# Three reorderings in a one-core spectral filter + MLP kernel: the load order of the row table, a subtraction given to GpSimd, and a copy put ahead of two splits

## The chip, the cores and the metric

The kernel runs on one core of a Trainium2 chip. The metric is the device time of one execution in microseconds (us), median over runs. The engines are TensorE (PE; its weight loads are shown apart as PEld), VectorE (DVE), ScalarE (ACT), GpSimd (POOL) and SyncE (SP, which here only issues DMAs). Each runs its own instruction queue in order and waits on semaphores for the others.

## What is computed

The input is x with 2048 rows (positions) of 576 features. A GFNet filter with a residual is followed by an MLP with a residual:

```python
def _A_ref(x, w_r, w_i):
    B, S, D = x.shape
    X = rfft2(x) * (w_r + 1j * w_i)
    return irfft2(X, s=(S, D))

def _B_ref(x, w1, w2):
    h = jnp.maximum(jnp.einsum("bsd,df->bsf", x, w1), 0)
    return jnp.einsum("bsf,fd->bsd", h, w2)

h = x + _A_ref(_layernorm(x), w_r, w_i)
h2 = h + _B_ref(_layernorm(h), w1, w2)      # w1 576 x 4608, w2 4608 x 576
```

## The kernel before

The work is laid out as one program whose order is written by hand: the tile framework runs in a manual schedule (L171), so that each engine gets its instructions in the order of the Python code, and only the semaphores between engines are worked out for it. x stands in 16 tiles of 128 rows. Matmuls run in a reduced fp32 form; where full precision is needed, an operand is split into a high part (a copy by ACT, L159) and a low part (a subtraction, v minus its high part), and three products are summed.

**Start and forward transform.** `load_x(xs, t, 1)` (L165 to L167) loads one tile in two halves: SP issues both, but for tiles 0 and 1 ACT issues the second. After tiles 0 and 1 SP loads the row table (`cc`, its first 192 columns, `caf` in the code, L173 to L176), then tiles 2 to 15 and the other tables. The first layer norm is folded in. Per tile, DVE makes the statistics (`stat1`, L242; `aggr1`, L246; `row1`, L250 and L251; `add1`, L263), POOL the power for 1/sqrt (`pow1`, L255) and one subtraction (L258), ACT scales the row table by it (`scale1`, L267 and L268), and PE multiplies (`fwd_a`).

**Inverse transform, second layer norm, projection and the first MLP steps.** These are interleaved by the string STEPS, one letter a call: `h` and `d` are the first matmuls of the inverse for a tile (their PSUM is folded by L159 on ACT and L536, L537 on DVE), `o` writes the folded rows (L543 on POOL, L544 on DVE), `r` is its row step, which takes two tiles together (r7 reads tiles 12 and 13), `e` adds the residual (L519, DVE), `s` and `n` are the second layer norm (statistics L215, L216 on DVE, L218 to L221 on POOL), and `j` is `project`. `A` is the first MLP product (A0 and A1 the two halves of its step 0), `B` the second. The part that matters reads

```python
"... j0 j1 h9 d8 s5 r4 n2 e6 o8 e7 d9 o9 j2 j3 h10 d10 r5 h11 e8 s6 e9 s7 s8 "
"n4 o10 d11 s9 o11 j4 A0 j5 h12 n6 A1 d12 r6 h13 e10 e11 d13 o12 j6 j7 B0 B1 o13 B2 =K0 s10 h14 n8 r7 ..."
```

`project(t)` transposes the normalised tile (PE, L564) into a PSUM bank. ACT copies the bank twice (both by L159): its high part into `dst`, the operand buffer of a chunk of four tiles (slots 0 to 5), and all of it into an SBUF buffer `zt`, which SP stores (L572). POOL subtracts twice for the low parts (L574, from `zt`, slots 6 to 9). 576 is 4 x 128 + 64, and the 64 left-over features stand in slot 2: rows 0 to 63 the high part, rows 64 to 127 the low part, made by L575 on DVE from the PSUM bank. After the fourth tile of a chunk SP copies rows of slot 2 to slot 5 within SBUF (L579, four copies: the first two read rows 32 to 63, the last two rows 96 to 127) and then rows 0 to 31 to rows 32 to 63 of slot 2 (L580). A product such as A0 has 14 matmuls; its last two read the slots 2 and 5.

PSUM has four wide banks in two pools of two; a string `order` says from which pool each new bank comes. A bank is free again when its last reader is done.

**Doubles.** From about 280 us the MLP runs as Strassen-Winograd products on pairs of chunks and weight groups. `slot(d)` has seven rounds r: PE makes one product of the next double's first layer (`l1_prod`, L825), and two products of this double's second layer (`second`, L930), whose results DVE adds (L940). Between them, `pieces` runs what the table PLAN names for a round and a place: `u2c` copies the first-layer bank into SBUF (ACT), `y1h` and `y1l` are the high and low part of the sums s1, s2 (ACT L159, DVE L839; the sums are made on POOL, L845 to L851), `y3h` and `y3l` the same of s3, s4. `weights(d, r)` splits and loads weights for the next turn: `w1_split("A2", nc.gpsimd)` has two copies on ACT (high and rest) and two subtractions on POOL (L353, L377), and `load_w1` issues DMAs. In the first double (d = 0, `late`) there is a plan of its own for the rounds 0 to 2.

Of the kernel before, what the change touches and what calls it, by code (L numbers as in the profile page):

```python
# [129 lines left out]
def kernel(ctx: ExitStack, tc: tile.TileContext, x, w_r, w_i, w1, w2, cc2, c1, fb, ib, c3, out):  # L130
    nc = tc.nc
# [6 lines left out]
    def sb(shape, tag, bufs=1, dt=F32):  # L138
        n[0] += 1
        return pool.tile(shape, dt, tag=tag, name=f"{tag}_{n[0]}", bufs=bufs)  # L140
# [6 lines left out]
    def ps():  # L147
        n[0] += 1
        return (wide if next(order) == "w" else psum).tile([128, 1024], F32, tag="d", name=f"d_{n[0]}", bufs=2)

    def ebuf(shape, dt=F32):
        e = sb([128, EW], "e", EB, dt)[:, :int(np.prod(shape[1:]))]
        return e.rearrange("p (a b) -> p a b", a=shape[1]) if len(shape) == 3 else e
# [4 lines left out]
    def act(o, i, **kw):  # L158
        nc.scalar.activation(o, i, AF.Copy, **kw)  # L159

    xs = sb([128, NT, D], "X")
# [3 lines left out]
    def load_x(xs, t0, k):  # L165
        for j in range(2):
            (nc.scalar if j and t0 < 2 else nc.sync).dma_start(xs[64 * j:64 * j + 64, t0:t0 + k, :], xv[j, :, t0:t0 + k, :])  # L167
# [2 lines left out]
    make_identity(nc, ident)  # L170
    ctx.enter_context(tc.manual_schedule())  # L171
    load_x(xs, 0, 1)
    load_x(xs, 1, 1)  # L173
    ccs = sb([128, 320], "cc")
    caf, cai = ccs[:, :192], ccs[:, 192:]
    nc.sync.dma_start(caf, cc2[:, :192])  # L176
    for i in range(2, NT):
        load_x(xs, i, 1)
    cst = ebuf([128, 1160])
# [151 lines left out]
    def load_w1(g, v1, v4):  # L331
        f = slice(256 * g, 256 * g + 256)
        nc.sync.dma_start(v1, w1[0:512, f].rearrange("(a p) f -> p a f", p=128))
        for k in range(3):
            nc.sync.dma_start(v4[32 * k:32 * k + 32], w1[512:576, f].rearrange("(h p) f -> p h f", p=32))
# [135 lines left out]
    xs = xa[:, :NT * D].rearrange("p (t d) -> p t d", t=NT)  # L471
# [88 lines left out]
    def project(t):  # L560
        y = Zs.pop(t)
        pz = ps()
        for b in range(5):
            nc.tensor.transpose(pz[:, 128 * ORDER[b]:128 * ORDER[b] + 128], y[:, 128 * b:128 * b + 128], ident)  # L564
        q = slice(128 * (t % CH), 128 * (t % CH) + 128)
        dst = xc[t // CH]
        pzv = pz[:, :640].rearrange("p (a s) -> p a s", s=128)
        act(dst[:, 0:5, q], pzv)
        zt = ebuf([128, 640])
        act(zt, pz[:, :640])  # L570
        xd[t] = dram.tile([128, 640], F32, name=f"x{t}")
        nc.sync.dma_start(xd[t], zt)  # L572
        for h in range(2):
            nc.gpsimd.tensor_sub(dst[:, 6 + 2 * h:8 + 2 * h, q], zt[:, 384 * h:384 * h + 256].rearrange("p (a s) -> p a s", s=128), dst[:, 3 * h:3 * h + 2, q])  # L574
        nc.vector.tensor_sub(dst[64:, 2, q], pzv[64:, 2], dst[64:, 2, q])  # L575
        if t % CH == CH - 1:
            u = dst.bitcast(F32)
            for a, b in ((0, 32), (32, 32), (64, 96), (96, 96)):
                nc.sync.dma_start(u[a:a + 32, 5], u[b:b + 32, 2])  # L579
            nc.sync.dma_start(u[32:64, 2], u[0:32, 2])  # L580
# [126 lines left out]
    def load_sum(p, n, back=False):  # L707
        if back:
            td[p, n] = dram.tile([128, 2560], F32, name=f"t{p}{n}")
        for at, v, m in zip((0, 384) if n != "B22" else (0, 1536), TF[n], (3, 2)):  # L710
            v = v.rearrange("p a n -> p (a n)").bitcast(F32)
            t = td[p, n][:, at:at + 512 * m]
            if n != "B22":
                v, t = v.rearrange("p (j n) -> p j n", j=4), td[p, n].rearrange("p (j n) -> p j n", j=4)[:, :, at:at + 128 * m]
            nc.sync.dma_start(*((t, v) if back else (v, t)))
# [37 lines left out]
    def w1_split(n_, eng):  # L753
        v, s_, v4 = vs[1], vs["s"], vs[4]
        if n_ == "A11":
            split(*W1["A11"][:2], v[:, 0:2, :128], eng)
            split_rest(W1["r"][:, 768:896], v4[:, 0, :128], nc.gpsimd)
        elif n_ == "A2":
            split(*(v2d(x) for x in W1["A2"]), v[:, 2:4, :], eng)
            split_rest(W1["r"][:, 512:768], v4[:, 1], eng)  # L760
        else:
            k = n_ == "S34"
            split(*W1[n_], s_[:, 512 * k:512 * k + 512], eng)
            split_rest(W1["r"][:, 256 * k:256 * k + 256], vs["r"][k], eng)
# [9 lines left out]
    def w2_sums():  # L774
        v, s_ = vs[2], vs["s"]
        b11, b12, b21, b22 = v[:, 0, :288], v[:, 0, 288:], v[:, 1, :288], v[:, 1, 288:]
        t1, t2, t3, t4 = (s_[:, 288 * k:288 * k + 288] for k in range(4))
        nc.gpsimd.tensor_sub(t1, b12, b11)
        nc.gpsimd.tensor_sub(t2, b22, t1)
        nc.gpsimd.tensor_sub(t3, b22, b12)  # L780
        nc.gpsimd.tensor_sub(t4, b21, t2)

    def w2_split(n_, eng):
        v, s_ = vs[2], vs["s"]
        if n_ == "B1":
            split(*W2["B1"], v[:, :, :288], eng)
        elif n_ == "B22":
            split(*W2["B22"], v[:, 1, 288:], eng)
        else:
            k = 576 * (n_ == "T34")  # L790
            split(*W2[n_], v2d(s_[:, k:k + 576]), eng)
# [16 lines left out]
    LAST = len(doubles) - 1  # L808
# [18 lines left out]
    def piece(d, n_):  # L827
# [73 lines left out]
    PLAN = {  # L901
# [7 lines left out]
    }  # L909
    PRE = "z3h yAh yc2"  # L910

    def pieces(d, names, first=False):
        for n_ in names.split():
            if first and (n_[0] == "y" or n_ in ("z1h", "z1l", "z3l")):
                continue
            piece(d, n_)
# [50 lines left out]
    def weights(d, r):  # L967

        g = doubles[max(d, 0)][0]
        turn = (d + 1) % 2  # L970
        if not turn and r == 0 and d > 0:
            w2_split("T34", nc.vector)
            w2_split("B22", nc.gpsimd)
        if g == NG - 1:
            return
        if turn:
            if r == 1:
                w1_split("A2", nc.gpsimd)
                if g + 2 < NG:
                    load_w1(g + 2, vs[1], vs[4])  # L980
            if r == 3:
                w2_sums()
            if r == 4:
                w2_split("B1", nc.gpsimd)
            if r == 5:
                w2_split("T12", nc.gpsimd)
            for n_, k in STREAM:
                if max(k, 2 * (d == 0)) == r:
                    load_sum(doubles[d + 2][1], n_)
        else:  # L990
            if r == (1 if d > 0 else 5):
                load_w2(g + 1, vs[2])
            if r == 1:
                w1_split("A11", nc.gpsimd)
            early = d < 0
            if r == 2 - early:
                w1_sums(0)
            if r == 3 - early:
                w1_sums(1)
            if r == 4 - early:  # L1000
                w1_split("S12", nc.gpsimd)
            if r == 5 + early:
                w1_split("S34", nc.gpsimd)

    def slot(d):
        pieces(d, PRE if d else "")
        late = not d
        for r in range(7):
            l1_prod(d + 1, (0, 2, 1)[r] if late and r < 3 else r)
            plan = PLAN.get((r, 0), "")  # L1010
            if late:
                plan = {0: "p1c z1h z1l", 1: "", 2: "u2c"}.get(r, plan)
            pieces(d, plan)
            if not late or r:
                second(d, 2 * r - late)
            pieces(d, PLAN.get((r, 1), ""))
            second(d, 2 * r + 1 - late)
            if late and r == 0:
                pieces(d, PRE)
            if late and r == 2:  # L1020
                split(*HF["Y"]["A11"], fx["p1"][0][:, :256])
            if late and r == 6:
                second(d, 13)
            pieces(d, PLAN.get((r, 2), "").replace("yBh yBl", "" if d == LAST - 1 else "yBh yBl"))
            weights(d, r)
            if d == LAST - 1 and r == 4:
                split(W1["S12"][0][:, :288], W1["S12"][1][:, :288], vs[2][:, 0, 288:], eng=nc.gpsimd)
            if d == LAST - 1 and r == 5:
                split(*HF["Y"]["S12"], fx["p1"][LAST % 2], eng=nc.gpsimd)
# [148 lines left out]
    for d in range(LAST):  # L1178
        slot(d)
# [23 lines left out]
```

## Time and profile before

| | us |
|---|---|
| median of 3 runs | 971.03 (971.01 to 971.31) |
| the profiled execution | 971.31 |
| its span, first to last instruction | 969.3 |
| PE busy in the span | 957.8 |
| DVE, ACT, POOL busy | 780.2, 464.4, 633.2 |

A row of the timeline gives start and duration in us, engine, line, operation, output <- input by buffer names, shapes, a count where neighbours were drawn together, and in brackets the idle time ahead of it with what ended it. A group's row gives busy us and mean ns, then the idle us ahead. A row with q behind the engine (SPq) is its DMA queue: the time that issuing took, not the transfer.

### The profile page before, as it was taken

What the parts mean: (1) busy time and instruction counts of PE and PEld (TensorE: products, weight loads), DVE (VectorE), ACT (ScalarE), POOL (GpSimd) and SP (SyncE); (2) the same over time, 40 slices, a digit from 0 to 9 for tenths busy, and PEclk for the clock granted to TensorE, in tenths of its full rate; (3) what the DMA queues carried; (4) which work ended last, traced back from release to release, by engine and by line L of the source; (5) the groups of instructions that cost most, each with busy time, mean ns of one, the idle gap of its engine ahead of it and who ended that gap; (6) DMA issues with size and microseconds to landing.
All of it is one profiled execution on the core that took longest, in us unless ns stands there. A gap on an engine that the chain in (4) does not pass through costs nothing.

```text
span 969.3 us, 18102 instructions
## 1 busy us (share of the span) xinstructions
PE 957.8 (99%) x6658; PEld 849.5 (88%) x6658; DVE 780.2 (80%) x1235; ACT 464.4 (48%) x912; POOL 633.2 (65%) x774
## 2 busy tenths in 40 slices
PE   8999999999999999999999999999999999999998
PEld 7777678899988999999999999999999999999997
DVE  8677976787858888888888888888888888888886
ACT  6544556333345454545454544444454554544441
POOL 7213755623777866777776878776777777686842
PEclk9999999999999999999999999999999999999999
DMA  7874735567559182645637181927355472809265
GB/s 208 227 191 111 176 102 192 184 221 250 199 167 313 45 295 84 242 144 183 202 124 264 63 301 43 308 65 262 122 204 181 147 242 84 298 30 325 95 216 158
DMA packets 122840, 176.09 MB, mean 182 GB/s; under 512 B 7552, under 2 KB 102400, under 8 KB 122752
## 3 DMA queue, kind: packets, MB, share of 16 engines
q1 hardware_dynamic: 121584, 173.61, 55.3%
q10 hardware_dynamic: 1168, 1.33, 0.4%
q8 instruction: 53, 0.87, 0.4%
q14 instruction: 35, 0.29, 0.1%
HBM read 150.53 MB, written 23.07 MB: 179 GB/s over the span
## 4 chain that ended last, share of the span: by engine, by line
PE 92%; DVE 4%; issue 1%; POOL 1%; ACT 1%; DMA 0%; DVEq 0%; POOLq 0%; ACTq 0%
PE h L825 35%; PE d L930 34%; PE d L156 22%; DVE A L519 1%; DVE st L215 1%; PE d L564 1%; DVE st L242 1%; PE h L930 0%; DVE e L536 0%; DVE e L537 0%; DMA X<-in_A_x_dram 0%; ACT e L159 0%; ACT X L159 0%; DVE X L544 0%; POOL e L353 0%
## 5 line engine op out<-in xcount | busy, mean ns | idle before, releaser
L940 DVE TENSOR_TENSOR A<-A,d 128x576 f32<-128x576 f32 x428 | 316.8, 752 | 80.1 <-PE d L930 67.7
L930 PE MATMUL d<-X,D 128*128 128x288 f32 x1476 | 224.2, 294 | 0.1
L930 PEld LDWEIGHTS d<-X,D 128*128 128x128 f32 x1476 | 211.0, 188 | 10.5 <-DVE A L940 0.3
L825 PE MATMUL h<-B,e 128*128 128x512 f32 x658 | 166.8, 392 | 0.0
L159 ACT ACTIVATE e<-h 128x512 f32<-128x512 f32 x93 | 55.6, 598 | 184.8 <-PE h L825 184.8
L825 PEld LDWEIGHTS h<-B,e 128*128 128x128 f32 x658 | 118.3, 188 | 20.3
L353 POOL TENSOR_TENSOR e<-e,e 128x512 fp32r<-128x512 f32 (+4 forms) x67 | 89.0, 1328 | 58.9 <-ACT e L159 58.8
L825 PE MATMUL h<-X,e 128*128 128x512 f32 x434 | 110.2, 393 | 1.0 <-ACT e L159 1.0
L641 ACT ACTIVATE e<-e 128x512 f32<-128x512 f32 x93 | 58.9, 634 | 105.8 <-DVE e L883 47.0
L353 POOL TENSOR_TENSOR X<-e,X 128x576 fp32r<-128x576 f32 (+1 forms) x34 | 50.0, 1471 | 63.7 <-ACT X L159 63.0
L825 PEld LDWEIGHTS h<-X,e 128*128 128x128 f32 x434 | 78.0, 188 | 14.6 <-ACT e L159 1.2
L159 ACT ACTIVATE e<-e 128x256 fp32r<-128x256 f32 (+5 forms) x171 | 78.8, 490 | 17.3 <-DVE e L672 6.1
L849 POOL TENSOR_TENSOR A<-e 128x256 f32<-128x256 f32 x61 | 48.1, 788 | 28.0 <-DVE X L839 19.9
L839 DVE TENSOR_TENSOR D<-A,D 128x512 fp32r<-128x512 f32 x61 | 64.8, 1062 | 1.7 <-ACT D L159 1.7
L930 PEld LDWEIGHTS d<-X 128*128 128x128 f32 x372 | 55.6, 188 | 5.3 <-issue 0.4
L930 PE MATMUL d<-X 128*128 128x288 f32 x372 | 58.9, 294 | 0.1
L930 PE MATMUL d<-X,e 128*128 128x288 f32 x360 | 57.1, 294 | 0.0
L825 PE MATMUL h<-F,e 128*128 128x512 f32 x217 | 55.0, 392 | 0.0
L156 PE MATMUL d<-e,D 128*128 128x288 f32 x384 | 53.3, 295 | 0.0
L825 PE MATMUL h<-C,e 128*128 128x512 f32 x210 | 53.3, 392 | 0.0
L851 POOL TENSOR_TENSOR A<-e,A 128x256 f32<-128x256 f32 x61 | 52.7, 863 | 0.8 <-DVE A L847 0.8
L156 PEld LDWEIGHTS d<-e,D 128*128 128x128 f32 x384 | 51.9, 188 | 1.3 <-issue 0.4
(174 smaller groups left out, 1850.6 us busy)
## 6 DMA issues: line engine op xcount, KB each, us to landing
X<-t0T SPq DMA_DIRECT2D x16, 768.0 KB
X<-t1T SPq DMA_DIRECT2D x16, 768.0 KB
e<-in_B_w_dram SPq DMA_DIRECT2D x18, 576.0 KB
e<-in_B_w_dram SPq DMA_DIRECT2D x18, 512.0 KB
X<-t0T SPq DMA_DIRECT2D x16, 512.0 KB
X<-t1T SPq DMA_DIRECT2D x16, 512.0 KB
B<-t1T SPq DMA_DIRECT2D x8, 768.0 KB
B<-t1B SPq DMA_DIRECT2D x8, 768.0 KB
```

Source lines behind the costliest of these rows:

```text
L156: nc.tensor.matmul(o, l, r, start=start, stop=stop)
L159: nc.scalar.activation(o, i, AF.Copy, **kw)
L215: nc.vector.bn_stats(st[:, i, h, :], xs[:, t0 + i, 288 * h:288 * h + 288])
L242: nc.vector.bn_stats(first(t)[2][:, h, :], xs[:, t, 288 * h:288 * h + 288])
L353: eng.tensor_sub(l, v, h)
L641: nc.scalar.activation(o, i, AF.Relu)
L825: nc.tensor.matmul(o, a, b, start=bool(first) and n_ == 0, stop=n_ == len(ops) - 1, skip_group_check=not first)
L839: (eng or nc.vector).tensor_sub(f[1], v, f[0])
L849: nc.gpsimd.tensor_sub(s3, p0[:, :256], p0[:, 256:])
L851: nc.gpsimd.tensor_sub(s4, p1_[:, :256], s2)
L930: nc.tensor.matmul(P[tt], l[:, q], r, start=first and n_ == 0, stop=end and n_ == 2, skip_group_check=whole and not first)
L940: nc.vector.tensor_add(xt, xt, P)
```

## The change

Three edits that compute the same values.

1. SP issues the row table ahead of tile 1's half, no longer behind it.
2. `project`'s L575 takes its input from the SBUF copy `zt` instead of the PSUM bank, for all 16 tiles; for tiles 0 to 7 it runs on POOL instead of DVE.
3. In the first double, `w1_split("A2")` (with `load_w1` behind it) moves from the end of round 1 to the end of round 2, and `y1h y1l` from the end of round 1 to round 2, behind `u2c`.

```diff
     load_x(xs, 0, 1)
-    load_x(xs, 1, 1)
     ccs = sb([128, 320], "cc")
     caf, cai = ccs[:, :192], ccs[:, 192:]
     nc.sync.dma_start(caf, cc2[:, :192])
+    load_x(xs, 1, 1)
...
-        nc.vector.tensor_sub(dst[64:, 2, q], pzv[64:, 2], dst[64:, 2, q])
+        (nc.gpsimd if t < 8 else nc.vector).tensor_sub(dst[64:, 2, q], zt[64:, 256:384], dst[64:, 2, q])
...
-            if r == 1:
+            if r == (1 if d else 2):
                 w1_split("A2", nc.gpsimd)
...
-                plan = {0: "p1c z1h z1l", 1: "", 2: "u2c"}.get(r, plan)
+                plan = {0: "p1c z1h z1l", 1: "", 2: "u2c y1h y1l"}.get(r, plan)
...
-            pieces(d, PLAN.get((r, 2), "").replace("yBh yBl", "" if d == LAST - 1 else "yBh yBl"))
+            if not late or r != 1:
+                pieces(d, PLAN.get((r, 2), "").replace("yBh yBl", "" if d == LAST - 1 else "yBh yBl"))
```

What this does to the queues, at two places. POOL in the projection, tiles 2 and 3 (e_1704 and e_1718 are their `zt`, B_1416 is `dst`), with the engine semaphores that each row waits for:

```order
 L574 TENSOR_TENSOR B_1416<-e_1704,B_1416 128x2x128 [waits Activation_49]
 L574 TENSOR_TENSOR B_1416<-e_1704,B_1416 128x2x128
-L574 TENSOR_TENSOR B_1416<-e_1718,B_1416 128x2x128 [waits Activation_49]
+L575 TENSOR_TENSOR B_1416<-e_1704,B_1416 64x128 [waits Pool_49]
+L574 TENSOR_TENSOR B_1416<-e_1718,B_1416 128x2x128 [waits Activation_49,Pool_49]
 L574 TENSOR_TENSOR B_1416<-e_1718,B_1416 128x2x128
-L218 TENSOR_SCALAR r_1761<-mv_1760 128x2 [waits DVE_49]
+L575 TENSOR_TENSOR B_1416<-e_1718,B_1416 64x128 [waits Pool_49]
+L218 TENSOR_SCALAR r_1761<-mv_1760 128x2 [waits DVE_49,Pool_49]
 L219 TENSOR_TENSOR r_1761<-r_1761,half_169 128x2 [waits Pool_49]
```

Each tile's L575 now stands behind its two L574 and waits for POOL's own earlier work; what follows on POOL stands behind it. The eight rows of L575 are gone from DVE's queue.

ACT in the first double (h_3270 is the bank that u2c, e_3208, copies; D_3422<-A_1399 is y1h; e_3205 and e_3206 are the two copies of the split A2; e_3420<-e_3208 is the split of A11 and e_3420<-A_1399 is y3h):

```order
 L641 ACTIVATE e_3295<-h_3269 128x512
-L159 ACTIVATE D_3422<-A_1399 128x512
-L159 ACTIVATE e_3205<-e_2775 128x512
-L159 ACTIVATE e_3206<-G_2777 128x256
-L159 ACTIVATE e_3208<-h_3270 128x512
-L159 ACTIVATE e_3420<-e_3208 128x256
-L159 ACTIVATE e_3420<-A_1399 128x512
+L159 ACTIVATE e_3208<-h_3270 128x512
+L159 ACTIVATE D_3422<-A_1399 128x512
+L159 ACTIVATE e_3420<-e_3208 128x256
+L159 ACTIVATE e_3420<-A_1399 128x512
+L159 ACTIVATE e_3205<-e_2775 128x512
```

The copy u2c went ahead of y1h, and the two copies of the split (e_3206 follows e_3205) behind y3h. PE, DVE and POOL have the same order there as before.

## The prediction, made before the change was run

> **What bounds the kernel now.** The page comes first: TensorE is busy for all but 11.5 us of the span, so only what makes it idle, or stops it from idling, counts.
>
> ```profile
> span 969.3 us, 18102 instructions
> ...
> PE 957.8 (99%) x6658; PEld 849.5 (88%) x6658; DVE 780.2 (80%) x1235; ACT 464.4 (48%) x912; POOL 633.2 (65%) x774
> ```
>
> Next the waits of PE (line waited for: us in total, times, longest). Each of the three edits has its own row here:
>
> ```profile
> PE d L156 <- ACT e L268: 1.7, 3, 1.1
> ...
> PE d L156 <- DVE B L575: 1.0, 2, 0.7
> PE h L825 <- ACT e L159: 1.0, 1, 1.0
> ```
>
> If every one of these went, 3.7 us would be won. The timeline of each place says how much of it can go. Times below are us from the span's start; the profiled execution took 971.31, 0.28 above the median of 971.03, and 2.0 of it lie outside the span. I work out differences and set them on the median.
>
> **Edit 1, the load order.** SP's queue, then ACT, DVE and PE around the first tiles:
>
> ```profile
> 0.74 1.48 SPq L167 DMA_DIRECT2D X<-in_A_x_dram  x2
> 2.26 0.59 SPq L176 DMA_DIRECT2D cc<-in_cc_dram  x1
> 2.90 1.10 SPq L167 DMA_DIRECT2D X<-in_A_x_dram  x2
> ```
> ```profile
> 6.40 0.46 ACT L268 ACTIVATE e<-cc,r 128x192 f32<-128x192 f32 x1 [0.45 <-DMA cc<-in_cc_dram]
> ```
> ```profile
> 6.13 0.82 DVE L242 BATCH_NORM_STATS2 st<-X 128x6 f32<-128x288 f32 x2
> ```
> ```profile
> 8.58 0.62 PE L156 MATMUL d<-e 64*128 64x128 f32 x6 [0.18 <-ACT e L268]
> ```
>
> The row table cc, issued third at 2.26, could be used at 6.40 (4.14 behind its issue) and held ACT for 0.45. Issued second it is there earlier, and ACT can gain at most those 0.45 for tile 0. They are not on the path: PE, which idles again (0.18) before tile 1, waits for tile 1's chain, and that runs through DVE: DVE's statistics at 6.13 run straight behind tile 0's work with no idle, so tile 1's data came just in time or earlier. Its second issue at 1.48 becomes the third at about 2.2. With cc's 4.14 it is usable at 6.40 instead of 6.13: every later link of the DVE chain is **0.28 late**, rounded up from 0.27 for its issue at 2.26. Bounds: tile 1 had landed long before 6.13 and nothing moves (0; no gain, for PE's idle ahead of tile 1 swallows tile 0's); or it takes the 6.13 − 1.48 = 4.65 that it may have taken before, usable at 6.85 (+0.72). I take the middle row, cc's own, which is the transfer that had this place in the queue.
>
> **Edit 2, what it frees.** L575 read PSUM, so the bank that project() fills came free when DVE had run L575. Now ACT's copies at L159 free it.
>
> ```profile
> 129.75 0.96 PE L156 MATMUL d<-B,F 128*128 128x512 f32 x3 [0.70 <-DVE B L575]
> ```
> ```profile
> 127.61 0.46 DVE L537 TENSOR_TENSOR e<-e,d 128x290 f32<-128x290 f32 x1
> ...
> 129.40 0.29 DVE L575 TENSOR_TENSOR B<-d,B 64x128 fp32r<-64x128 f32 x1
> ```
> ```profile
> 119.31 1.91 PE L156 MATMUL d<-e,X 64*64 64x290 f32 x16 [0.24 <-DVE A L519]
> ```
>
> At 129.75 the second product of MLP step 0 (A1) waits for tile 4's L575, which stood in DVE's queue until 129.40. Without it the last reader of that bank is L537, done at 128.07, and PE could start when its matmuls of 128.33 are through, about 128.88: **−0.87**. The other wait on L575 (1.0 − 0.7 = 0.3, near 115.4) gains nothing: PE next waits at 119.31 for L519, which the change leaves where it was.
>
> **Edit 2, what it costs on GpSimd.** The trace has no 64x128 subtraction on POOL; the nearest groups are
>
> ```profile
> L749 POOL TENSOR_TENSOR e<-e,G 128x128 f32<-128x128 f32 x16 | 7.7, 482 | 1.3
> ...
> L377 POOL TENSOR_TENSOR e<-G,e 32x128 fp32r<-32x128 f32 x16 | 7.2, 453 | 1.3
> ```
>
> so 0.47 each, and 0.10 for the wait on POOL's own L574 that now stands ahead of it: 0.57, where DVE took 0.29. Two places read what comes behind.
>
> *The rest operands of A0.* Tiles 0 to 3 in POOL's order, then SP's copies of the leftover rows, their bytes (GB/s in slices of 0.1 us from 124.0), and the 14 weight loads of A0:
>
> ```profile
> 113.96 3.01 POOL L574 TENSOR_TENSOR B<-e,B 128x256 fp32r<-128x256 f32 x4
> 117.70 0.23 POOL L218 TENSOR_SCALAR r<-mv 128x2 f32<-128x2 f32 x1 [0.73 <-DVE mv L216]
> ...
> 120.26 0.90 POOL L543 TENSOR_TENSOR X<-e 128x287 f32<-128x287 f32 x1 [0.27 <-DVE e L537]
> 121.12 2.79 POOL L574 TENSOR_TENSOR B<-e,B 128x256 fp32r<-128x256 f32 x4
> ```
> ```profile
> 121.49 2.53 SPq L579 DMA_DIRECT2D B<-B  x4
> 124.21 0.98 SPq L580 DMA_DIRECT2D B<-B  x1
> ```
> ```profile
> GB/s 143 184 225 62 0 0 102 184 266 62 41 0 21 0 20 0 0 0 143 205 225 82 0 0 0 0 0 0 333 384 410 410 410 384 384 410 154 0 0 0
> ```
> ```profile
> 124.35 3.07 PEld L156 LDWEIGHTS d<-B,F 128*128 128x128 f32 x14
> ```
>
> Tiles 0 and 1: L574 ends at 116.97, two L575 make it 118.1, 0.4 past L218's 117.70; the idle 0.27 ahead of L543 takes up most, and tile 2's L574 starts at 121.2. Then 1.4 + 0.57 + 1.4 + 0.57: tile 3's L575 ends at 125.2, where DVE's was done before the copies began at 121.49. Copies 1 and 2 of L579 don't read it; copy 3 does, and on SP copy 4 and L580 are queued behind it: issues at 125.25 and 125.85 (0.63 each), L580 from 126.5 to 127.05. Before, L580's issue ended at 125.19, its bytes moved at 125.8 to 126.2, and A0's last weight load (3.07/14 = 0.22 each, so at 127.2) did not wait: it lands 1.0 to 2.0 behind its issue. I take 1.4, nearer the bytes: 128.45. A0's last two matmuls then wait **1.25**, from 127.2. Behind them come 0.45 of their own, 0.64 of transposes and 0.6 up to A1: 130.15 against 129.75. Stall and gain together: **+0.40** (bounds −0.87, copies in time, to +1.2: 2.0 behind the issue and 0.2 of contention).
>
> *The inverse's row step r7*, which reads tiles 12 and 13. POOL (L574 of tiles 6 and 7, L543 of tile 13), then PE:
>
> ```profile
> 139.00 2.84 POOL L574 TENSOR_TENSOR B<-e,B 128x256 fp32r<-128x256 f32 x4 [2.45 <-ACT e L159]
> 141.79 0.70 POOL L543 TENSOR_TENSOR X<-e 128x287 f32<-128x287 f32 x1
> ```
> ```profile
> 143.34 0.67 PE L156 MATMUL d<-X,cc 64*64 64x288 f32 x8
> ```
>
> Two L575 (1.14) and the new wait move L543 to 143.1, its end to 143.85; the matmuls that read it started at 143.34: **+0.50** (bounds 0, at 0.3 for a L575, to +1.1 at L574's 0.71 and more). PE had no other wait between 130 and 290, so nothing gives it back. The eight L575 that stay on DVE read two SBUF tiles; ACT held them up before, DVE idles behind most of them: 0 (up to +0.5).
>
> **Edit 3, the first double's round 2.** PE, ACT, POOL, DVE:
>
> ```profile
> 286.58 1.78 PE L825 MATMUL h<-X,e 128*128 128x512 f32 x7
> ...
> 289.00 0.95 PE L930 MATMUL d<-X 128*128 128x288 f32 x6
> 290.90 1.43 PE L825 MATMUL h<-X,e 128*128 128x512 f32 x5 [0.95 <-ACT e L159]
> ```
> ```profile
> 295.81 0.95 PE L930 MATMUL d<-X,e 128*128 128x288 f32 x6
> ```
> ```profile
> 288.91 0.64 ACT L159 ACTIVATE D<-A 128x512 fp32r<-128x512 f32 x1 [2.89 <-POOL A L847]
> ...
> 290.28 0.57 ACT L159 ACTIVATE e<-h 128x512 f32<-128x512 f32 x1
> ```
> ```profile
> 290.22 1.74 POOL L353 TENSOR_TENSOR e<-e,e 128x512 fp32r<-128x512 f32 x1
> 292.04 0.73 POOL L377 TENSOR_TENSOR e<-G,e 32x256 fp32r<-32x256 f32 x1
> ```
> ```profile
> 289.58 1.23 DVE L839 TENSOR_TENSOR D<-A,D 128x512 fp32r<-128x512 f32 x1 [0.99 <-ACT D L159]
> ...
> 292.25 0.81 DVE L353 TENSOR_TENSOR e<-e,e 128x256 fp32r<-128x256 f32 x1
> 292.98 1.29 DVE L839 TENSOR_TENSOR e<-A,e 128x512 fp32r<-128x512 f32 x1
> ...
> 294.79 1.41 DVE L940 TENSOR_TENSOR A<-A,d 128x576 f32<-128x576 f32 x2
> ```
>
> The copy u2c (290.28) had its input at 288.36, but stood behind y1h, which waited for POOL, and two splits. Put first it is done at 289.0, and PE's product of 290.90 follows its last one at 289.8: 1.1 won there. The splits come at 290.9 and 291.4 instead, so POOL's subtractions end near 294.0; the next but one product (A12), then at 293.1, needs them at its third and seventh matmul, 293.6 and 294.5: just in time. But y1h still waits for POOL, so DVE's chain from 289.58 does not move, and the additions of 294.79 (0.70 each) free the bank for PE's 295.81. They end at 295.5, or 295.3 if the two additions ahead close up: of the 1.1 about **−0.48** is left (bounds −1.1 to +0.2). What load_w1 fetches behind the splits leaves 1.2 later and is read a slot later.
>
> **A rule against the trace.** POOL's 292.04 + 0.73 = 292.77; DVE's L353 at 292.25 took 0.81, ending 0.29 behind that (a 64x128 one took 0.29 at 129.40): as if it had waited for POOL's to end. The Trainium skill, SBUF — State Buffer, section Who interferes with whom, says that a DVE instruction with two SBUF inputs and a GpSimd one that reads SBUF exclude each other for a whole instruction; these rows agree, and by that rule the sum would be the lock's below.
>
> **Sum.** +0.28 + 0.40 + 0.50 − 0.48 = +0.70: 972.0 for the profiled execution, 971.03 + 0.70 = **971.7** for the median. About 0.2% (1.94) is what a measurement of this kernel can tell from no change.
>
> **Rivals.**
> - *The copies come in time* (0.20): L575 on POOL takes 0.3, or the tail of A0 needs its rows later than I read. For it: DVE's 0.29; against: the POOL groups. Then, with every other bound on its near side, 0 for the load, −0.87 at A1, 0 at r7, −1.1 for edit 3: −1.97, 969.1.
> - *POOL becomes the bound of the projection, slower* (0.15): its L575 cost 0.75, as much as a whole L574 (121.12: 0.70 each), because DVE's additions read SBUF beside them. POOL's chain ahead of A0 then grows by 4 × 0.28 = 1.1, of which A0 gets 0.95 and the L543 ahead of r7 0.56: +0.28 + 1.35 + 1.06 − 0.48 = +2.2, 973.2. It decides from 0.7 per L575 on.
> - *The lock* (0.15): POOL's later subtraction (291.5 to 292.8, then 0.73) stands in front of DVE's 292.25 and 292.98; these end 0.1 to 0.2 later than before, the bank comes free at 295.7, edit 3 saves 0.1: +1.08, 972.1.
> - That the change doesn't do what it says is no rival: the order shows all three moves.
>
> **Chances.** Forecast 0.50, rivals as given. Faster by over 0.2% is half of the first rival and a little: 0.11; slower most of the second: 0.12; the same 0.77. The range reaches to both outer rivals and leaves their tails out: 969.0 to 973.3.
>
> **What would show it.** Right: no PE wait on L575; a new one of 1.0 to 1.5 ahead of A0's last two matmuls near 127; one of 0.5 on POOL's L543 near 143; DVE's second L242 pair at 6.4; PE's 290.90 product about 1.1 sooner and its L930 of 295.81 waiting for DVE. Wrong: no wait near 127 (A0's rest rows in time), L575 on POOL far from 0.47, or a wait in 147 to 184, where PE had none.

## The result, and the profile after

The changed kernel takes 972.87 us (median of 22 runs, 972.49 to 973.44) against 971.35 (22 runs) before: a ratio of 1.0017, 95% interval 1.0011 to 1.0023, so 1.5 us longer. The profiled execution took 972.79, with a span of 971.0, 1.7 longer than that of before. One execution in all runs below, 1914.76 us in the run of edit 2 alone, is left out of its ratio; nothing on record shows why it took so long.

The waits of PE, in the order of the page for before (line waited for: us in total, times, longest):

```profile
PE d L156 <- ACT e L268: 1.6, 3, 0.8
PE d L299 <- POOL ident masks.py:199: 1.4, 1, 1.4
PE d L156 <- DMA B<-B: 1.1, 1, 1.1
PE d L156 <- DVE e L537: 0.8, 2, 0.6
PE d L930 <- DVE A L940: 0.5, 1, 0.5
```

The rows of L575 (1.0) and of the bank that ACT frees for L825 (1.0) are gone, as the change meant; a wait for a DMA (1.1) and one for a VectorE addition (0.5) have come in. PE's idle as a whole did not grow (span less busy is 971.0 − 959.6 = 11.4, before 11.5), yet the span did, by 1.7: some of the new waits are waits of the weight loads (PEld, rows below) in the middle of a run of matmuls, and there PE shows a longer run, not idle. So I compare where the same matmul starts in the two traces. The shift of PE against before, in us, ahead of and behind each place:

| place (time before) | shift ahead | shift behind | difference |
|---|---|---|---|
| start to 110 | 0 | −0.03 | −0.03 |
| up to A0 and A1, 110 to 130 | −0.03 | +0.95 | +0.98 |
| row step r7, 143 to 146 | +0.94 | +1.59 | +0.65 |
| 146 to 200 (+0.12 at 157, −0.11 near 169) | +1.59 | +1.59 | 0 |
| plain MLP steps, 200 to 285 | +1.59 | +1.81 | +0.22 |
| first double, 285 to 299 | +1.81 | +1.71 | −0.10 |
| 299 to the end | +1.71 | +1.71 | 0 |

**A0.** POOL, SP, the weight loads and PE after:

```profile
115.63 0.46 POOL L575 TENSOR_TENSOR B<-e,B 64x128 fp32r<-64x128 f32 x1
...
118.22 0.42 POOL L218 TENSOR_SCALAR r<-mv 128x2 f32<-128x2 f32 x1
...
121.52 1.43 POOL L574 TENSOR_TENSOR B<-e,B 128x256 fp32r<-128x256 f32 x2
123.03 0.46 POOL L575 TENSOR_TENSOR B<-e,B 64x128 fp32r<-64x128 f32 x1
123.56 1.42 POOL L574 TENSOR_TENSOR B<-e,B 128x256 fp32r<-128x256 f32 x2
125.06 0.47 POOL L575 TENSOR_TENSOR B<-e,B 64x128 fp32r<-64x128 f32 x1
```
```profile
121.01 5.68 SPq L579 DMA_DIRECT2D B<-B  x4
126.80 0.53 SPq L580 DMA_DIRECT2D B<-B  x1
```
```profile
121.61 0.43 PEld L156 LDWEIGHTS d<-X,cc 64*64 64x64 f32 x9 [0.30 <-POOL X L543]
```
```profile
124.78 2.99 PE L156 MATMUL d<-B,F 128*128 128x512 f32 x12
128.87 0.71 PE L156 MATMUL d<-B,F 128*128 128x512 f32 x2 [1.10 <-DMA B<-B]
129.41 0.71 PE L564 MATMUL d<-ident,e 128*128 128x128 f32 x5
130.05 0.72 PE L156 MATMUL d<-e,X 64*64 64x290 f32 x8
130.70 0.50 PE L156 MATMUL d<-B,F 128*128 128x512 f32 x1
```

These L575 on POOL take 0.46 to 0.47. SP's four copies now span 5.68 instead of 2.53: the third had to wait for tile 3's L575, which ended at 125.53. L580's issue ended at 127.33, and 12 of A0's 14 matmuls were through when the last two waited until 128.87, 1.5 behind that issue. A1 starts at 130.70 instead of 129.75. A0 itself had started 0.43 late: tile 1's L575 had pushed the L543 ahead of it, which ended at 121.56 instead of 121.16, and a row step's weight loads waited 0.30 for it. The wait for the copies swallows that here.

**r7.** POOL, the weight loads and PE after:

```profile
143.51 0.55 POOL L575 TENSOR_TENSOR B<-e,B 64x128 fp32r<-64x128 f32 x1
144.14 0.70 POOL L543 TENSOR_TENSOR X<-e 128x287 f32<-128x287 f32 x1
```
```profile
144.89 0.67 PEld L156 LDWEIGHTS d<-X,cc 64*64 64x64 f32 x10 [0.46 <-POOL X L543]
```
```profile
144.27 1.80 PE L156 MATMUL d<-X,cc 64*64 64x288 f32 x16
146.00 1.91 PE L156 MATMUL d<-e,X 128*128 128x145 f32 x16
```

L543 starts 2.35 later than before (141.79), PE's matmuls only 0.93 later, which is PE's own shift, but the last ten of their 16 weight loads stood behind a wait of 0.46 for L543. The run spans 1.80 where the same 16 took 1.15 before.

**The eight L575 that stayed on VectorE** (tiles 8 to 15). The row step at 156.50, before and then after:

```profile
156.50 1.22 PE L156 MATMUL d<-X,cc 64*64 64x288 f32 x16
```
```profile
158.09 1.33 PE L156 MATMUL d<-X,cc 64*64 64x288 f32 x16
```

It starts with PE's shift of 1.59 and takes 0.11 more. PE's shift grows by 0.11 to 0.13 here in all six kernels of this text in which these tiles read the SBUF copy, and by 0.01 at most in the six others; no row shows which wait passes it on. Three of the eight (at 169.35, 174.40 and 182.76) stood beside work of POOL and took 0.87, 0.69 and 0.99 instead of 0.29; no wait of PE for VectorE follows them before 200.

**The first double.** PE, DVE and POOL after:

```profile
291.61 1.78 PE L825 MATMUL h<-X,e 128*128 128x512 f32 x7
...
297.40 1.06 PE L930 MATMUL d<-X,e 128*128 128x288 f32 x6 [0.52 <-DVE A L940]
```
```profile
294.08 0.86 DVE L353 TENSOR_TENSOR e<-e,e 128x256 fp32r<-128x256 f32 x1
294.86 1.22 DVE L839 TENSOR_TENSOR e<-A,e 128x512 fp32r<-128x512 f32 x1
296.01 0.67 DVE L875 TENSOR_TENSOR e<-e,h 128x512 f32<-128x512 f32 x1
296.60 1.41 DVE L940 TENSOR_TENSOR A<-A,d 128x576 f32<-128x576 f32 x2
```
```profile
293.36 1.30 POOL L353 TENSOR_TENSOR e<-e,e 128x512 fp32r<-128x512 f32 x1 [1.26 <-ACT e L159]
```

Take 1.81 off, PE's shift ahead of the double: the product of 290.90 starts at 289.80, 1.1 sooner, while DVE's addition starts at 294.79, just where it did. L930, which waits for the first of those two additions, comes at 295.59 instead of 295.81.

### The profile page after: what moved, and what is told of

Same layout as the page of the kernel before. It is cut to its first block, busy times and chain, and to the rows that moved or that the text cites. A ratio compares the mean times of both kernels' runs of the same rounds, so it can differ in the third digit from the quotient of the medians.

```text
span 971.0 us, 18106 instructions
## 1 busy us (share of the span) xinstructions
PE 959.6 (99%) x6658; PEld 849.7 (88%) x6658; DVE 779.0 (80%) x1227; ACT 463.8 (48%) x912; POOL 638.5 (66%) x782
## 4 chain that ended last, share of the span: by engine, by line
PE 92%; DVE 4%; POOL 2%; issue 1%; ACT 1%; DMA 1%; SPq 0%; DVEq 0%; POOLq 0%
PE h L825 35%; PE d L930 34%; PE d L156 22%; PE d L564 1%; DVE st L242 1%; PE h L930 0%; POOL B L574 0%; DVE A L519 0%; DMA X<-in_A_x_dram 0%; DVE st L215 0%; ACT e L159 0%; ACT X L159 0%; DVE e L537 0%; DVE e L536 0%; DVE A L940 0%
## 5 line engine op out<-in xcount | busy, mean ns | idle before, releaser
L940 DVE TENSOR_TENSOR A<-A,d 128x576 f32<-128x576 f32 x428 | 316.6, 751 | 80.1 <-PE d L930 67.6
L930 PE MATMUL d<-X,D 128*128 128x288 f32 x1476 | 224.2, 294 | 0.1
L930 PEld LDWEIGHTS d<-X,D 128*128 128x128 f32 x1476 | 211.0, 188 | 10.6 <-DVE A L940 0.3
L825 PE MATMUL h<-B,e 128*128 128x512 f32 x658 | 166.8, 392 | 0.0
L825 PEld LDWEIGHTS h<-B,e 128*128 128x128 f32 x658 | 118.3, 188 | 20.4
L353 POOL TENSOR_TENSOR e<-e,e 128x512 fp32r<-128x512 f32 (+4 forms) x67 | 88.7, 1324 | 60.4 <-ACT e L159 60.4
L825 PE MATMUL h<-X,e 128*128 128x512 f32 x434 | 110.1, 393 | 0.0
L353 POOL TENSOR_TENSOR X<-e,X 128x576 fp32r<-128x576 f32 (+1 forms) x34 | 50.0, 1473 | 62.1 <-ACT X L159 61.8
L825 PEld LDWEIGHTS h<-X,e 128*128 128x128 f32 x434 | 78.0, 188 | 13.4
L930 PEld LDWEIGHTS d<-X 128*128 128x128 f32 x372 | 55.6, 188 | 5.3 <-issue 0.4
L930 PE MATMUL d<-X 128*128 128x288 f32 x372 | 58.9, 294 | 0.1
L930 PE MATMUL d<-X,e 128*128 128x288 f32 x360 | 57.2, 294 | 0.5 <-DVE A L940 0.5
L825 PE MATMUL h<-F,e 128*128 128x512 f32 x217 | 55.0, 392 | 0.0
L825 PE MATMUL h<-C,e 128*128 128x512 f32 x210 | 53.2, 392 | 0.0
```

Of the source, the lines that this page charges most:

```text
L353: eng.tensor_sub(l, v, h)
L825: nc.tensor.matmul(o, a, b, start=bool(first) and n_ == 0, stop=n_ == len(ops) - 1, skip_group_check=not first)
L930: nc.tensor.matmul(P[tt], l[:, q], r, start=first and n_ == 0, stop=end and n_ == 2, skip_group_check=whole and not first)
L940: nc.vector.tensor_add(xt, xt, P)
```

## The experiments

All are compared with runs of the kernel before on the same chip; shifts are of PE's row, read as above.

**The three edits one by one.** First the load order alone.

```diff
     load_x(xs, 0, 1)
-    load_x(xs, 1, 1)
...
     nc.sync.dma_start(caf, cc2[:, :192])
+    load_x(xs, 1, 1)
```

> Edit 1 alone. Theory (tile 1's data has slack behind its new place in the queue): DVE's second pair of L242 stays at 6.1, the scaled row table L268 comes at 6.2 instead of 6.4, PE's idle ahead of tile 1 takes that up, and the time is that of before within 0.1. Rival (the step of the forecast): tile 1 lands where the row table landed, the second pair comes at 6.4 and the time is 0.28 longer.

Measured: 971.25 against 971.33, ratio 0.9999 (0.9991 to 1.0008). ACT and DVE of this run:

```profile
6.16 0.46 ACT L268 ACTIVATE e<-cc,r 128x192 f32<-128x192 f32 x1 [0.29 <-POOL r L255]
```
```profile
6.02 0.82 DVE L242 BATCH_NORM_STATS2 st<-X 128x6 f32<-128x288 f32 x2
```

Tile 1's statistics follow the chain of tile 0 with no idle, as before; tile 1 had slack. ACT's wait for the table became a shorter one for POOL's power. The theory held.

The rest subtraction alone (the line of L575 as in the change):

> Edit 2 alone. Theory (the whole loss of the change is this edit's, from GpSimd's queue): A0's last two matmuls wait over 1.2 for the copies of the rest rows, A1 starts 1.0 later than before, the row step r7 ends 0.6 later still, together +1.6 us and no other place over 0.3. Rival (the forecast's sizes): +0.9. Rival (the three edits act on each other, so that the loss is not the edit's own): less than +0.5.

Measured: 972.68 against 971.33, ratio 1.0017 (1.0008 to 1.0026). PE:

```profile
128.65 0.71 PE L156 MATMUL d<-B,F 128*128 128x512 f32 x2 [1.07 <-DMA B<-B]
```

The shift grows by 0.97 at A0 and A1 and by 0.66 at r7, as in the changed kernel; no other place has over 0.35, and those shifts differ between executions (last section). By the medians the edit costs 1.35 of the 1.52, and neither of the others costs anything: the loss is this edit's.

The first double alone (its three places as in the change):

> Edit 3 alone. Theory (VectorE's chain behind the high part y1h, which waits for GpSimd, does not move, and PE wins only what its L930 of 295.81 stood behind that chain's addition): the L825 product of 290.90 comes 1.1 sooner, L930 waits for L940, net -0.2 to -0.3. Rival (the forecast's size, the two additions close up): -0.5. Rival (the chain is no bound): -1.1.

Measured: 971.00 against 971.33, ratio 0.9996 (0.9988 to 1.0005). PE's shift goes from −0.40 ahead of the double to −1.56 at the product of 290.90 and is back at −0.52 behind L930: 0.12 won.

```profile
295.16 1.06 PE L930 MATMUL d<-X,e 128*128 128x288 f32 x6 [0.50 <-DVE A L940]
```

**Without GpSimd.** All 16 L575 read the SBUF copy, on VectorE:

```diff
-        nc.vector.tensor_sub(dst[64:, 2, q], pzv[64:, 2], dst[64:, 2, q])
+        nc.vector.tensor_sub(dst[64:, 2, q], zt[64:, 256:384], dst[64:, 2, q])
```

> Before, with L575 of all tiles reading the SBUF copy, but all on VectorE. Theory (the gain is in the bank that comes free with ACT's copy, the loss in GpSimd's queue): PE's wait at 129.75 for L575 goes, the copies of the rest rows leave as before, no wait near 127 or 143, about -0.87 us. Rival (a VectorE subtraction with two SBUF inputs waits for GpSimd's L574 beside it, and what is behind it on VectorE comes late): the gain is under 0.4 or a new PE wait on VectorE stands between 110 and 184.

Measured: 971.37 against 971.33, ratio 1.0000 (0.9991 to 1.0009); the theory fell and its rival held. A1's wait did go (A1 at 129.72 behind a shift of +0.75, so 0.78 won), but PE had lost 0.8 before it. DVE of before, then DVE, POOL and PE of this run:

```profile
115.04 0.50 DVE L575 TENSOR_TENSOR B<-d,B 64x128 fp32r<-64x128 f32 x2
```
```profile
114.98 1.45 DVE L575 TENSOR_TENSOR B<-e,B 64x128 fp32r<-64x128 f32 x2
```
```profile
113.90 3.12 POOL L574 TENSOR_TENSOR B<-e,B 128x256 fp32r<-128x256 f32 x4
```
```profile
119.05 0.77 PE L564 MATMUL d<-ident,e 128*128 128x128 f32 x5 [0.76 <-DVE A L519]
```

Two L575 that read PSUM took 0.50 at 115.04; now they stand beside POOL's L574 and take 1.45, and what is behind them on VectorE, L519, comes late. A run for this alone has the SBUF copy for tiles 0 and 1 only:

```diff
+        nc.vector.tensor_sub(dst[64:, 2, q], zt[64:, 256:384] if t < 2 else pzv[64:, 2], dst[64:, 2, q])
```

> Before, with L575 of tiles 0 and 1 reading the SBUF copy, all on VectorE. Theory (a VectorE subtraction with two SBUF inputs and GpSimd's L574 with SBUF inputs exclude each other): the two L575 at 115.0 take 1.4 to 1.5 instead of 0.5, VectorE is 0.8 late from there on, PE waits 0.8 for L519 near 118.4, and the wait at 129.75 stays: +0.8 us. Rival (what cost 0.8 with all tiles on VectorE was another tile's L575): the two take 0.6, under +0.2.

Measured: 971.98 against 971.19, ratio 1.0011 (1.0002 to 1.0020). The theory held: the two L575 take 1.45, and PE's shift goes from −0.01 at 110 to +0.81 at 119:

```profile
115.03 1.45 DVE L575 TENSOR_TENSOR B<-e,B 64x128 fp32r<-64x128 f32 x2
```
```profile
PE d L564 <- DVE A L519: 0.8, 1, 0.8
PE d L156 <- DVE B L575: 0.7, 1, 0.7
```

So for these tiles the SBUF copy as an input has a price on either engine: a place in GpSimd's queue, or a wait for GpSimd on VectorE.

**Which tiles.** The changed kernel with tiles 0 to 3, then with tiles 6 and 7, put back on VectorE and PSUM:

```diff
-        (nc.gpsimd if t < 8 else nc.vector).tensor_sub(dst[64:, 2, q], zt[64:, 256:384], dst[64:, 2, q])
+        if t < 4:
+            nc.vector.tensor_sub(dst[64:, 2, q], pzv[64:, 2], dst[64:, 2, q])
+        else:
+            (nc.gpsimd if t < 8 else nc.vector).tensor_sub(dst[64:, 2, q], zt[64:, 256:384], dst[64:, 2, q])
```

> The changed kernel, with L575 of tiles 0 to 3 put back on VectorE, reading PSUM as before. Theory (tiles 0 to 3 on GpSimd make A0's stall, tile 4 makes the gain, tiles 6 and 7 make r7's loss): no wait near 127, A1 at 128.9, the shift of 0.6 at 144 stays: -0.85 + 0.65 - 0.1 = -0.3 against before. Rival (A0 waits for its copies whatever makes the rest rows): A1 later than 129.7.

Measured: 971.59 against 971.19, ratio 1.0004 (0.9995 to 1.0013). No wait for the copies; A1 at 129.26, a shift from +0.17 to −0.49, so 0.66 won; then +0.64 at r7 and −0.13 in the double. The mechanism held, the sum did not: it is zero by the trace and +0.40 by the medians (no clear change), not −0.3, since A1 won 0.2 less and, in the profiled execution, the start was 0.2 late.

```diff
-        (nc.gpsimd if t < 8 else nc.vector).tensor_sub(dst[64:, 2, q], zt[64:, 256:384], dst[64:, 2, q])
+        if t in (6, 7):
+            nc.vector.tensor_sub(dst[64:, 2, q], pzv[64:, 2], dst[64:, 2, q])
+        else:
+            (nc.gpsimd if t < 8 else nc.vector).tensor_sub(dst[64:, 2, q], zt[64:, 256:384], dst[64:, 2, q])
```

> The changed kernel, with L575 of tiles 6 and 7 put back on VectorE, reading PSUM as before. Theory (two L575 and their waits on GpSimd push the L543 ahead of r7): the 16 matmuls of r7 run through again, the shift of 0.6 at 144 goes, that at 129 stays (+1.0): +0.9 against before, 0.6 under the changed kernel. Rival (r7 is late by what VectorE does with its two SBUF inputs, L544, not by GpSimd's queue): the shift at 144 stays within 0.2.

Measured: 972.56 against 971.21, ratio 1.0013 (1.0004 to 1.0022). PE:

```profile
144.44 1.15 PE L156 MATMUL d<-X,cc 64*64 64x288 f32 x16
```

r7 runs through, and the shift stays +1.11 from 133 to 146: that loss was the queue's. But the time is +1.35 against the changed kernel's +1.52, no clear gain. The profiled execution, 973.14, is the slowest of the 11: in it PE lost 0.66 between 200 and 285 (+1.25 to +1.91), where by the trace's releasers its weight loads waited 0.23 for GpSimd near 239, 0.23 for VectorE (L638 of before) near 252 and 0.39 for a DMA load near 272. The changed kernel lost 0.22 there and the run of edit 3 alone 0.27; the runs with the edit of L575 alone and with the other copy order (next) lost 0.02. So it is no fixed price of any edit; what decides it stays open.

**SP's queue.** The changed kernel, with L580 ahead of the last two copies:

```diff
-            for a, b in ((0, 32), (32, 32), (64, 96), (96, 96)):
+            for a, b in ((0, 32), (32, 32)):
                 nc.sync.dma_start(u[a:a + 32, 5], u[b:b + 32, 2])
             nc.sync.dma_start(u[32:64, 2], u[0:32, 2])
+            for a, b in ((64, 96), (96, 96)):
+                nc.sync.dma_start(u[a:a + 32, 5], u[b:b + 32, 2])
```

> The changed kernel, with L580 ahead of the third and fourth copy of L579 in SP's queue (L580 reads and writes nothing that L575 makes). Theory (A0 waits for the last of three transfers that are issued one after the other behind L575): L580 leaves at 122.3, the last copy's issue ends at 126.7 instead of 127.3, A0's two matmuls start 0.6 sooner, +0.9 against before. Rival (the landing of the copies, or L575 itself, sets the wait, and not the queue): under 0.2 gained.

Measured: 973.40 against 971.21, ratio 1.0023 (1.0013 to 1.0032), slower still. SP, then PE at A0 and at the same place of the third chunk:

```profile
120.98 1.26 SPq L579 DMA_DIRECT2D B<-B  x2
125.24 0.51 SPq L580 DMA_DIRECT2D B<-B  x1
125.83 1.18 SPq L582 DMA_DIRECT2D B<-B  x2
```
```profile
128.54 0.47 PE L156 MATMUL d<-B,F 128*128 128x512 f32 x1 [0.57 <-DMA B<-B]
```
```profile
171.14 0.47 PE L156 MATMUL d<-C,F 128*128 128x512 f32 x1 [1.18 <-DMA C<-C]
```

At A0 it won 0.6 (A1 at 130.14), but not as I had it. L580 overwrites rows that the first two copies read, so it waited for them to land, until 125.24, 3.0 behind the end of their issue, and the last two copies behind it were issued 0.3 later than in the changed kernel. What helped is that the last copy no longer had L580 behind it: the last issue that A0 waits for ended at 127.01 instead of 127.33, and one matmul of A0 instead of two stood behind it. In the third chunk, where L575 never was late, L580's wait now held up the last two copies, and PE lost 1.2 at a place where it had lost nothing.

**The gains alone.** Tile 4 alone reads the SBUF copy, on VectorE:

```diff
+        nc.vector.tensor_sub(dst[64:, 2, q], zt[64:, 256:384] if t == 4 else pzv[64:, 2], dst[64:, 2, q])
```

> Before, with L575 reading the SBUF copy for tile 4 alone, all on VectorE. Theory (A1's bank is the only place where L575 held PE for good; every other tile gains nothing by the change): PE's wait at 129.75 goes, A1 starts at 128.9, nothing else moves, -0.85 us. Rival (another reader of that bank or VectorE's next work is late there, so that the wait only changes its name): A1 at 129.4 or later, under 0.35 gained.

Measured: 970.42 against 971.21, ratio 0.9994 (0.9985 to 1.0002). PE and DVE:

```profile
127.98 0.72 PE L156 MATMUL d<-e,X 64*64 64x290 f32 x8
128.63 2.56 PE L156 MATMUL d<-B,F 128*128 128x512 f32 x10
```
```profile
129.03 0.29 DVE L575 TENSOR_TENSOR B<-e,B 64x128 fp32r<-64x128 f32 x1
```

A1 follows with no idle; the shift goes from −0.37 to −1.12. POOL ran no L574 then, and this L575 took 0.29. The low part y3l behind the addition of round 3's first second-layer product, on top of edit 3:

```diff
+            if late and r == 2:
+                pieces(d, "y3h")
...
+            if late and r == 3:
+                pieces(d, "y3l")
             second(d, 2 * r + 1 - late)
```

> Before with edit 3, and the low part y3l (L839) on VectorE put behind the next addition L940 instead of ahead of L875. Theory (L930 of the next round waits for that addition, and y3l, 1.2 long beside GpSimd, stands in front of it): the addition ends 1.2 sooner, L930 doesn't wait any more, about -0.9 against before where edit 3 alone gave -0.2 in its place. Rival (L930 or the product ahead of it waits for the split A2 on GpSimd as well): under 0.3 more than edit 3 alone.

Measured: 970.59 against 971.21, ratio 0.9994 (0.9985 to 1.0003). In its place 0.64 is won (−0.02 to −0.66) where edit 3 alone won 0.12, less than the 0.9 expected. DVE and PE:

```profile
293.61 0.74 DVE L940 TENSOR_TENSOR A<-A,d 128x576 f32<-128x576 f32 x1
294.27 0.85 DVE L839 TENSOR_TENSOR e<-A,e 128x512 fp32r<-128x512 f32 x1
```
```profile
294.88 0.95 PE L930 MATMUL d<-X,e 128*128 128x288 f32 x6
```

L930 no longer waits; the rest of the 1.1 goes in smaller waits near 291.5 and 295.8 (weight loads waited 0.7 for L940 in two places). Both together:

> The two gains that stood alone, together: L575 of tile 4 from the SBUF copy, the rest from PSUM, all on VectorE; edit 3 with y3l behind the next addition; the load order of before. Theory (they are in different places of PE's row, with no idle between that could swallow one): the sum, -0.75 and -0.65, is -1.4 us. Rival (VectorE's chain, now nearer to PE, gives part of it back): -0.8 or less.

Measured: **969.79** against 971.19 (969.35 to 970.01), ratio 0.9986 (0.9977 to 0.9995): the sum, −1.4. By the trace −0.77 at A1, −0.60 in the double, and 0.2 near 169 that most of the other runs show too against the one profiled execution of before. This beats both kernels.

## Why the prediction was right, and where it was off

Forecast was +0.70, measured +1.5: the range held it, "within 0.2%" is where it ended, and the likeliest case (the costs of edit 2 on GpSimd eat the gains) is the one that the runs show. The cost is over twice the forecast, though, and a wrong term helped the number: without the +0.28 of edit 1 the sum would have been +0.42. "About 0.2%" as what can be told from no change was too wide here: the interval of 0.11% to 0.23% leaves no doubt of the loss. By its steps:

- **Edit 1, +0.28: wrong, 0.** The step "tile 1 is usable where the row table was" failed: of its two bounds the near one held (the second pair of L242 stayed at 6.09 after). No row of before showed when tile 1 landed, only that it was not late.
- **A1's bank, −0.87: right.** Alone it gave −0.75. That the other wait on L575 (115.4) is swallowed at 119.31 held too: the changed kernel is 0.48 ahead at 117 and level again at 119.
- **A0's rest operands, net +0.40: the mechanism right, the size 0.58 short.** L575 cost 0.46 as taken. The chain was 0.3 later than added up: I let the idle ahead of L543 swallow tile 0's and 1's delay, but L218, 0.23 long before, took 0.42, and tile 2's L574 began at 121.52 instead of 121.2. L580's issue so ended 0.28 later, the landing took 1.54 instead of 1.4, and from the last two matmuls to A1 it was 1.83 instead of 1.70.
- **r7, +0.50: right**, +0.65. The wait of 0.5 for L543 is there, 0.46, on the weight loads. L543 ended at 144.84, which less PE's shift of 0.94 is 143.90; the forecast had 143.85. One of the two L575 took 0.55.
- **The eight L575 left on VectorE, 0 (up to +0.5): about +0.12**, at the row step of 156.50. In the table the −0.11 near 169 cancels it, where the weight loads waited 0.36 for the third chunk's copies before and 0.26 after.
- **Edit 3, −0.48: the mechanism right, the size short.** DVE's chain behind y1h bounds L930, but "the two additions ahead close up" did not happen (they took 1.60 for two again), so only the 0.3 was left that L930 had stood behind the addition: 0.22 by its start and 0.10 behind the double.
- **Not forecast: +0.22** between 200 and 285, which two of the other runs show and the rest don't.

Of the rivals, the one with GpSimd's cost at 0.75 had a total nearer to the result (+2.2), but its reason is refuted (0.46). The lock's number for edit 3 (0.1 saved) was met, but not by its account: that DVE's chain would end 0.1 to 0.2 later. It ended where it did before. The lock fits the trace: after, POOL's L353 ran from 293.36 for 1.30, and DVE's L353 of 294.08 ended at 294.94, 0.28 behind it; before, the same instruction took 0.81 and ended 0.29 behind another of POOL's. Moving the split only changed the partner. What I did not see is that the lock bears on edit 2 more than on edit 3: left on VectorE, the two L575 of tiles 0 and 1 took 1.45 instead of 0.50 beside L574, and PE lost there what tile 4 won. The Trainium skill (SBUF — State Buffer, Who interferes with whom) says it in full, that a VectorE instruction with two SBUF inputs and a GpSimd instruction that reads SBUF exclude each other; 1.45 against 0.50 beside L574, and 0.29 for tile 4, when GpSimd ran no L574, agree with it.

## What to carry to other kernels

A wait that is removed at sixteen places was worth something at one (tile 4, 0.75 us); edit that place, and leave the other fifteen as they were. Before an operation is moved to a slower engine, follow everything that is queued behind it there, to the DMAs that read its result and the DMAs behind those. Where a copy is put first to free an engine, ask which chain ends last afterwards: here an unhurried subtraction ahead of the addition kept most of the gain, and moving it behind gave 0.5 more.

## What the runs showed of the hardware

A VectorE subtraction of 64 x 128 takes 0.29 us with one input in PSUM or with both in SBUF, but with both in SBUF and beside GpSimd's subtractions two of them took 1.45. On GpSimd it takes 0.46 to 0.47, once 0.55. A DMA of 32 rows of 2 KB from SBUF to SBUF was usable 1.5 us behind the end of its issue at A0; with the other copy order L580 had to wait for one until 3.0 behind it. Single executions also differ where their kernels are alike. This is DVE near the end of the start, in the kernel before and with edit 3 alone, which have the same program there:

```profile
16.68 1.14 DVE L263 SCALAR_TENSOR_TENSOR e<-X,r 128x288 f32<-128x288 f32 x1
```
```profile
16.53 0.50 DVE L263 SCALAR_TENSOR_TENSOR e<-X,r 128x288 f32<-128x288 f32 x1
```

The short one is followed by a shift of PE that is 0.33 smaller from there on. So two profiles are compared place by place, and a difference of their spans under half a microsecond says little.
